# In-place block products in a gated linear attention scan, and a weight check ordered behind the last unit's masks

## The chip, the cores and the metric

The kernel runs on one core of one Trainium2 chip. The metric is device time in microseconds (us): 799.12 us is the median of five runs of the kernel before (797.18 to 802.22). The engines are named as in the profile: PE (matmul), PEld (its weight loads), DVE (the vector engine), ACT (the scalar engine), POOL and SP (here used mostly to issue DMAs).

## The reference

A gated linear attention with a complex decay gives `x`, and a feed-forward block with a squared ReLU follows.

```python
mag = sqrt(a_re**2 + a_im**2); scale = min(mag, 0.999) / (mag + 1e-6)
ar, ai = a_re * scale, a_im * scale            # (B, H, S, D) = (4, 8, 768, 48)
for t in range(S):                             # state (B, H, D, D), complex
    S_re, S_im = ar[t]*S_re - ai[t]*S_im + outer(k[t], v[t]), ar[t]*S_im + ai[t]*S_re
    y[t] = q[t] @ S_re
x = y.transpose(0, 2, 1, 3).reshape(3072, 384)
out = maximum(x @ w_in, 0)**2 @ w_out          # w_in 384 x 2048, w_out 2048 x 384, float64
```

The two weight matrices arrive as 64-bit floats and are lowered to float32 on the chip.

## The kernel before, in words

**Units.** The 3072 rows are cut into 8 units of 384 rows (4 batches, 2 halves each), `u["n"]` 0 to 7. Each unit passes three stages.

- `chain_work`: loads `a`, `q`, `k`, `v`; normalises the gates (`roots`, `normalise`); multiplies them within groups of 3 rows (`inner`, 128 groups per unit); `totals` transposes the 128 group products with PE (tile `tot`) into the tile `e`, which is 128 partitions by (2 parts, 3 chunks of channels, 129 places). `scan` then turns the 128 places into running complex products. `back` transposes them back with PE (tile `bk`), ACT copies them to `xn`, and `apply` multiplies them into the gates, giving `QK`.
- `pair_work`: for each of 4 pairs of heads `turn` (PE transposes `tq`, ACT copies to `QKT`), `score` (PE `sa`, DVE multiplies by the mask into `A`), `keep` (PE `kv`, DVE sums the states into `St` and `S`), `mix` (PE `ypair`, ACT copies to `yt`, SP issues the DMAs into `xT`).
- `hidden_work` (PE `h`, ACT squares into `g`) and `project_work` (PE `o`, ACT copies to `ot`, SP stores).

**The scan before** (lines 814 to 838). `product` (line 796) is one complex multiplication in four DVE operations: two multiplications over both parts (line 808) into the scratch tiles `fa0`, `fa1`, one subtraction (811), one addition (812). `scan` views the 128 places as 32 blocks of 4. Three products make the running products inside the blocks (`v4`, stride of 4 elements in memory). The 32 block ends are copied into a small tile (`inc`, line 822) and scanned there: three products inside 8 groups of 4, three doubling steps over the 8 group ends, three products (one per chunk) to bring the group ends in. Three more products, again one per chunk, multiply all 4 places of blocks 1 to 31 by the end of the block before. That is 15 products and a copy: 61 operations. One unit in two adds a small carry product into `ce`.

**The weight check.** The range of the 64-bit weights is checked in 32 pieces during the last unit's dense stage. `look(i)` issues a DMA of a piece (384 KB) through POOL into one of four scratch tiles; `inspect(i)` masks its high words (line 635) and takes their maximum (line 637), then calls `look(i + 4)`. `verdict` gathers all checks; one PE matmul (`cnt`, line 1058) and one DVE operation make the flag that decides, at the very end, whether a slower general path has to run.

**Order.** `merge` interleaves the lists of work of neighbouring units: the dense stage of unit n, the pairs of unit n+1, the chain of unit n+2. What is written there is only a priority: a scheduler with its own estimates of durations sets the order of the instructions on every engine when the program is built, and each engine then runs its own queue strictly in that order. `after(x, y)` adds an order between two instructions to that scheduler and no semaphore. The first unit has no stage before it, so its chain runs alone at the start.

## Time and profile before

The profiled execution took 795.03 us, with a span of 793.3 us from the first to the last instruction, at a mean granted TensorE clock of 0.991.

| engine | busy us | share of the span | instructions |
|---|---|---|---|
| PE | 716.8 | 90% | 3538 |
| PEld | 467.2 | 59% | 3538 |
| DVE | 517.4 | 65% | 1340 |
| ACT | 400.7 | 51% | 754 |
| POOL | 110.3 | 14% | 162 |

Busy shares are averages over stages with different limits: PE does almost nothing in the first 40 us, then is nearly full. A row of the timeline reads: start, duration in us, engine, line, operation, output and input tiles, their sizes, and in brackets the idle time before it with what ended it. One fp32 matmul of the program appears as two records in the trace.

### The profile page before, as it was taken

How to read it: one execution, taken by the hardware profiler on the slowest of the kernel's cores; microseconds unless marked ns; L12 is line 12 of the kernel's file. 1: busy time of each engine (PE TensorE's matmuls, PEld its weight loads, DVE VectorE, ACT ScalarE, POOL GpSimd, SP SyncE). 2: the span in 40 equal slices, each digit the busy share in tenths (PEclk: the TensorE clock that was granted, in tenths of full speed). 3: DMA queues.
4: the chain of work that ended last, by engine and by line, in shares of the span. 5: the costliest groups of instructions: out<-in, count | busy, mean ns of one | idle time of the engine just before them, and what ended most of it. 6: DMA issues, size and time to landing. Idle time of an engine off the chain costs nothing.

```text
span 793.3 us, 10047 instructions
## 1 busy us (share of the span) xinstructions
PE 716.8 (90%) x3538; PEld 467.2 (59%) x3538; DVE 517.4 (65%) x1340; ACT 400.7 (51%) x754; POOL 110.3 (14%) x162
## 2 busy tenths in 40 slices
PE   0169799899899999999999999999899999899997
PEld 0047455567455666766566666666566666565553
DVE  5899889887988985688654858287655867510000
ACT  5825388067667439911993149621982145212510
POOL 4004100031040022002300050003200144100000
PEclk9999999999999999999999999999999999999999
DMA  9429440061051034003600071004500188500000
GB/s 277 161 69 321 139 148 11 14 226 45 16 199 51 26 112 162 9 19 93 210 8 9 29 236 30 16 18 130 167 8 18 58 275 285 169 18 28 0 11 25
DMA packets 38748, 76.25 MB, mean 96 GB/s; under 512 B 10752, under 2 KB 25216, under 8 KB 38688
## 3 DMA queue, kind: packets, MB, share of 16 engines
q0 software_dynamic: 14608, 55.85, 21.4%
q1 hardware_dynamic: 24080, 19.67, 8.3%
q8 instruction: 30, 0.49, 0.3%
q14 instruction: 30, 0.25, 0.1%
HBM read 56.62 MB, written 14.16 MB: 89 GB/s over the span
## 4 chain that ended last, share of the span: by engine, by line
PE 31%; issue 21%; DVE 8%; DMA 7%; ACT 7%; POOL 1%; SPq 0%; POOLq 0%; ACTq 0%
PE o L1012 15%; PE h L998 8%; DMA a<-in_a_im_dram 3%; PE sa L927 2%; DVE fa L808 2%; DMA look<-in_moe_w_out_dram 2%; PE ypair L963 1%; PE ypair L968 1%; PE kv L944 1%; DMA look<-in_moe_w_in_dram 1%; ACT QKT L918 1%; PE tq L917 1%; DMA rows<-QK 1%; ACT fa L677 1%; ACT g L1003 1%
## 5 line engine op out<-in xcount | busy, mean ns | idle before, releaser
L998 PE MATMUL h<-xT,w 128*128 128x384 f32 x768 | 265.1, 489 | 5.2 <-DMA xT<-yt 4.7
L1012 PE MATMUL o<-w,g 128*128 128x384 f32 x768 | 266.6, 492 | 0.0
L998 PEld LDWEIGHTS h<-xT,w 128*128 128x128 f32 x768 | 139.2, 191 | 87.5 <-issue 8.9
L1012 PEld LDWEIGHTS o<-w,g 128*128 128x128 f32 x768 | 140.8, 192 | 84.1 <-issue 4.9
L918 ACT COPY QKT<-tq 96x512 f32<-96x512 f32 x96 | 78.6, 855 | 28.3 <-PE tq L917 28.3
L1003 ACT ACTIVATE g<-h 128x384 f32<-128x384 f32 x128 | 61.7, 484 | 61.0 <-PE h L998 60.6
L1004 ACT ACTIVATE g<-g 128x384 f32<-128x384 f32 x128 | 66.6, 522 | 2.3
L929 DVE TENSOR_TENSOR A<-sa,mask 128x384 f32<-128x384 f32 x64 | 35.4, 553 | 44.9 <-PE sa L927 44.4
L917 PE MATMUL tq<-ident,QK 128*96 128x128 f32 x384 | 57.6, 278 | 6.0 <-ACT QKT L918 5.7
L917 PEld LDWEIGHTS tq<-ident,QK 128*96 128x96 f32 x384 | 44.4, 129 | 29.0 <-issue 11.8
L927 PEld LDWEIGHTS sa<-QKT 96*128 96x128 f32 x384 | 50.5, 193 | 17.1 <-ACT QKT L918 8.1
L927 PE MATMUL sa<-QKT 96*128 96x128 f32 x384 | 56.1, 284 | 4.7 <-ACT QKT L918 4.6
L1016 ACT COPY ot<-o 128x384 f32<-128x384 f32 x24 | 11.4, 474 | 86.9 <-PE o L1012 84.6
L971 ACT COPY yt<-ypair 112x384 f32<-112x384 f32 x32 | 15.3, 477 | 77.3 <-PE ypair L968 70.9
L1059 DVE TENSOR_SCALAR flag<-cnt 1x1 int32<-1x1 f32 x1 | 0.1, 148 | 68.4 <-PE cnt L1058 68.4
L779 PE MATMUL tot<-ident,last 128*128 128x128 f32 x72 | 14.4, 301 | 29.8 <-ACT last L739 26.2
L963 PE MATMUL ypair<-A,v 128*48 128x128 f32 x384 | 39.1, 282 | 0.3 <-ACT yt L971 0.3
L663 POOL DMA_DIRECT2D v<-in_v_dram x18 | 16.0, 893 | 156.4 <-issue 122.8
L896 POOL DMA_DIRECT2D rows<-QK x16 | 9.2, 574 | 203.8 <-DVE QK L888 164.7
L944 PEld LDWEIGHTS kv<-v,KC 128*96 128x96 f32 x320 | 31.6, 167 | 8.6 <-ACT QKT L918 4.0
L677 ACT ACTIVATE fa<-a 128x1152 f32<-128x1152 f32 x16 | 18.6, 1160 | 35.2 <-DMA a<-in_a_im_dram 35.2
L944 PE MATMUL kv<-v,KC 128*96 128x48 f32 x320 | 32.5, 248 | 2.7 <-DMA KC<-rows 1.5
(117 smaller groups left out, 964.1 us busy)
## 6 DMA issues: line engine op xcount, KB each, us to landing
rows<-QK POOLq DMA_DIRECT2D x16, 576.0 KB, 4.9
raw<-in_moe_w_in_dram POOLq DMA_DIRECT2D x16, 384.0 KB, 6.1
look<-in_moe_w_in_dram POOLq DMA_DIRECT2D x16, 384.0 KB, 4.1
look<-in_moe_w_out_dram POOLq DMA_DIRECT2D x16, 384.0 KB, 4.3
KC<-rows POOLq DMA_DIRECT2D x8, 576.0 KB, 5.0
out_dram<-ot SPq DMA_DIRECT2D x24, 192.0 KB, 1.9
raw<-in_moe_w_out_dram SPq DMA_DIRECT2D x11, 384.0 KB, 3.9
xT<-yt SPq DMA_DIRECT2D x48, 72.0 KB, 2.2
```

What stands on the lines that cost most here:

```text
L663: get.dma_start(out=u["v"][:, j], in_=src(v).rearrange("h (j s) d -> s j h d", s=C)[:, j])
L677: square = act.activation(out=whole(fa), in_=whole(a), func=AF.Square, accum_out=sums[:, n, z:z + 1])
L917: nc.tensor.transpose(ps[:, 2 * j + h], src, ident)
L918: act.copy(out=u["T"][i].rearrange("r z (p c) -> r c z p", c=W)[:, c], in_=ps)
L927: nc.tensor.matmul(sa[:, j], lhsT=T[:, 2 + h, ts(j, C)], rhs=T[:, h, ts(j, C)], start=True, stop=True)
L929: dve.tensor_tensor(out=u["A"][i][:, h], in0=sa, in1=mask3, op=ALU.mult)
L944: nc.tensor.matmul(ps[:, j, h], lhsT=u["KC", hh // HH][:, j, hh % HH], rhs=u["v"][:, j, hh], start=True, stop=True)
L963: nc.tensor.matmul(ypair[64 * h:64 * h + D, ts(j, C)], lhsT=u["v"][:, j, 2 * i + h], rhs=A[:, h, j], start=True, stop=S_j is None)
L998: nc.tensor.matmul(ps, lhsT=w1[:, f, m], rhs=u["xT"][:, m], start=(m == 0), stop=(m == NM - 1))
L1003: act.activation(out=t, in_=ps, func=AF.Relu)
L1004: act.activation(out=t, in_=t, func=AF.Square)
L1012: nc.tensor.matmul(u["o"], lhsT=u["g"][f][:, ts(c, C)], rhs=w2[:, f], start=(f == 0), stop=(f == NF - 1))
```

## The change

There are three edits. The scan is done in place in `e`, without `inc`: a first product joins blocks of 4 to blocks of 8 (16 block ends, a stride of 8 elements), four doubling steps run over the 16 ends, one product repairs the 16 left ends, and one product over all three chunks multiplies the first 3 places of blocks 1 to 31 by the end of the block before. That last product has too many dimensions for one operand, so its multiplications are issued per part: 4 multiplications, a subtraction and an addition. Together that is 42 operations. Second, the first operation of every `inspect` is ordered behind the last mask multiplication and the last state sum that were recorded. Third, for unit 0 the copy of the first state (4 copies, one per pair of heads) is done by ACT and not by DVE.

```diff
         hi = looks.pop(i)
-        dve.tensor_scalar(out=hi, in0=hi, scalar1=0x38000000, scalar2=0x78000000,
+        first = dve.tensor_scalar(out=hi, in0=hi, scalar1=0x38000000, scalar2=0x78000000,
                           op0=ALU.bitwise_xor, op1=ALU.bitwise_and)
+        for x in ("A", "S"):
+            after(first, mark[x])
...
-            dve.tensor_tensor(out=t, in0=x, in1=y[:, j].unsqueeze(1).to_broadcast(shape),
-                              op=ALU.mult)
+            if len(shape) < 5:
+                dve.tensor_tensor(out=t, in0=x, in1=y[:, j].unsqueeze(1).to_broadcast(shape),
+                                  op=ALU.mult)
+            else:
+                for r in range(2):
+                    dve.tensor_tensor(out=t[:, r], in0=x[:, r], in1=y[:, j], op=ALU.mult)
...
         for w in range(1, 4):
             product(u, v4[:, :, :, :, w], v4[:, :, :, :, w - 1], v4[:, :, :, :, w])
-        inc = whole(u["fb", 0])[:, 0:2 * NM * 32].rearrange("p (r m g) -> p r m g", r=2, m=NM)
-        i4 = inc.rearrange("p r m (k w) -> p r m k w", w=4)
-        dve.tensor_copy(out=inc, in_=v4[:, :, :, :, 3])
-        for w in range(1, 4):
-            product(u, i4[:, :, :, :, w], i4[:, :, :, :, w - 1], i4[:, :, :, :, w])
-        top = i4[:, :, :, :, 3]
-        for step in (1, 2, 4):
-            product(u, top[:, :, :, step:8], top[:, :, :, step:8], top[:, :, :, 0:8 - step])
-        for m in range(NM):
-            product(u, i4[:, :, m, 1:8, 0:3], i4[:, :, m, 1:8, 0:3],
-                    top[:, :, m, 0:7].unsqueeze(3).to_broadcast([C, 2, 7, 3]))
-        for m in range(NM):
-            product(u, v4[:, :, m, 1:32], v4[:, :, m, 1:32],
-                    inc[:, :, m, 0:31].unsqueeze(3).to_broadcast([C, 2, 31, 4]))
+        v8 = e[:, :, :, 0:C].rearrange("p r m (g w) -> p r m g w", w=8)
+        left, right = v8[:, :, :, :, 3], v8[:, :, :, :, 7]
+        product(u, right, right, left)
+        for step in (1, 2, 4, 8):
+            product(u, right[:, :, :, step:16], right[:, :, :, step:16],
+                    right[:, :, :, 0:16 - step])
+        product(u, left[:, :, :, 1:16], left[:, :, :, 1:16], right[:, :, :, 0:15])
+        product(u, v4[:, :, :, 1:32, 0:3], v4[:, :, :, 1:32, 0:3],
+                v4[:, :, :, 0:31, 3].unsqueeze(4).to_broadcast([C, 2, NM, 31, 3]))
...
-        dve.tensor_tensor(out=u["A"][i][:, h], in0=sa, in1=mask3, op=ALU.mult)
+        mark["A"] = dve.tensor_tensor(out=u["A"][i][:, h], in0=sa, in1=mask3, op=ALU.mult)
...
-            if before is None:
+            if before is None and u["n"] == 0:
+                act.copy(out=outs[j], in_=ps[:, j])
+            elif before is None:
                 dve.tensor_copy(out=outs[j], in_=ps[:, j])
             else:
-                dve.tensor_tensor(out=outs[j], in0=ps[:, j], in1=before, op=ALU.add)
+                mark["S"] = dve.tensor_tensor(out=outs[j], in0=ps[:, j], in1=before,
+                                              op=ALU.add)
```

The order that the scheduler makes of the changed program differs in these places. On DVE all 32 inspections now follow the last unit's last state sum. On PE the queue differs up to unit 3 and is the same from there to the end, `cnt` included (in front of the last 8 `o` matmuls of the program). In unit 1 the transposes `tot` and `bk` stand further back in the row of `o` matmuls (10 in place of 4 before the first `tot`, 35 in place of 31 before the first `bk`), and the six `bk` of `e` stand together, where before other matmuls lay between them; in unit 2 the first `bk` of `e` stands 1 matmul earlier. In unit 0 two and not three `h` matmuls stand before the last `ypair`. On POOL one `look` moves from in front of the last `KC` load to behind it. On ACT the four copies of unit 0 stand among the `raw` conversions.

## The prediction

> **What bounds the kernel now.** I read the busy table and the slices first, then the stretches of 20 us, the waits of PE, and around each of its waits the timelines of DVE and PE.

> ```profile
> PE   0169799899899999999999999999899999899997
> PEclk9999999999999999999999999999999999999999
> ```

> PE is nearly full from the fourth slice (60 us) to the end, so it bounds the kernel from there, and DVE counts only where PE waits for it. Before that it is idle. The stretches (columns: PE, PEld, DVE, ACT, POOL busy with counts, granted clock, DMA share, GB/s) show who is not:

> ```profile
> 20.00:40.00 20.00, 2.94 (x9) 1.48 (x9) 17.98 (x55) 16.20 (x31) 0.60 (x2) 1.00 0.48 156
> 40.00:60.00 20.00, 14.10 (x56) 9.75 (x57) 18.62 (x59) 5.57 (x10) 0.54 (x1) 1.00 0.25 78
> 140.00:160.00 20.00, 17.59 (x60) 10.85 (x59) 17.09 (x66) 1.82 (x4) 1.50 (x2) 0.91 0.11 35
> 680.00:700.00 20.00, 17.70 (x81) 11.10 (x80) 7.33 (x19) 4.46 (x7) 1.17 (x2) 0.91 0.28 92
> ```

> DVE bounds the start: unit 0's scan runs alone. In 140 to 160 and 680 to 700 PE has holes at a clock of 0.91. PE's waits (total, times, longest) and timeline name them:

> ```profile
> PE bk L844 <- DVE e L811: 19.1, 6, 12.4
> PE ypair L968 <- DVE St L954: 2.3, 1, 2.3
> ```
> ```profile
> 148.05 0.66 PE L844 MATMUL bk<-ident,e 128*128 128x128 f32 x2 [2.41 <-DVE e L811]
> 148.50 1.49 PE L1012 MATMUL o<-w,g 128*128 128x384 f32 x2
> ...
> 683.57 0.60 PE L968 MATMUL ypair<-QKT,St 96*48 96x128 f32 x4 [2.29 <-DVE St L954]
> ...
> 684.95 3.90 PE L1012 MATMUL o<-w,g 128*128 128x384 f32 x8
> ...
> 689.36 2.75 PE L1012 MATMUL o<-w,g 128*128 128x384 f32 x8
> ```

> `bk` waits for the end of a scan: 12.4 us at the start, 2.41 at 148, 2.53 at 213, 0.60 at 276; for units 4 to 7 PE reaches `bk` after the scan is done and waits for nothing. At 681 PE waits 2.29 us for a state sum that stands on DVE behind inspections, which wait for `look` DMAs; the next eight `o` records then take 3.90 us in place of 2.75.

> **The scan, step by step.** Rows of DVE by form (busy us, mean ns):

> ```profile
> L808 DVE TENSOR_TENSOR fa<-e 128x192 f32<-128x192 f32 x48 | 22.5, 504 | 13.0 <-ACT e L781 12.5
> L808 DVE TENSOR_TENSOR fa<-e,fb 128x248 f32<-128x248 f32 x48 | 17.8, 412 | 0.7
> L808 DVE TENSOR_TENSOR fa<-fb 128x42 f32<-128x42 f32 x64 | 10.6, 208 | 1.1
> L808 DVE TENSOR_TENSOR fa<-fb 128x48 f32<-128x48 f32 x48 | 9.7, 239 | 0.7
> ```

> Operands that lie together: 248 elements 412 ns, 576 elements about 751 ns (line 735), so 1.03 ns per element, 443 ns for 279. Operands in steps of 4 elements (16 bytes): 48 take 239 ns, 192 take 504, so 1.84 ns per element. The outputs in such steps (line 811: 96 elements 334 ns, 24 elements 201) grow by 1.85. Runs of 3 out of 4 pay nothing extra: the 42 mix both kinds, 229 ns in the doubling steps and 200 in runs of 3, as 1.84 and 1.03 per element would give.

> No row shows a step of 8 elements (32 bytes), which 24 of the new operations have. The lower bound of its price is that of operands lying together (1.03), the upper one the 16-byte price with its surcharge doubled (2.65); I take 1.84, the nearest row. [...]

> A product takes two multiplications and two half-size operations, less 0.12 us of overlap; with 48 elements 2 x 0.239 + 0.201 + 0.195 - 0.12 = 0.75, and the timeline has 0.76 (36.59 to 37.35). New: the join of 96 elements 1.02, steps of 90, 84, 72, 48 elements 0.99, 0.95, 0.89, 0.75, the left ends (90) 0.99: 5.59 us. The last product: four multiplications of 279 elements, 4 x 0.443 - 0.21 = 1.56, subtraction 0.36, addition 0.45: 2.37. Together 7.96. Old, same place: from the copy at 36.23 to the end of the last addition at 46.77, 10.54. Saved: 2.6 us per scan. The steps of 8 hold 1440 elements, so the high price saves 1.4 and the low one 3.7.

> **What it moves.** *Start:* all of unit 0 hangs on this chain. `bk` of the real part now waits for the one subtraction, and six `bk` come together, some 0.2 us: 2.4 us earlier.

> *Unit 0's pairs, 62 to 96 us:* DVE (18.66 and 16.70 of 20 busy) loses four copies of 0.25 us. ACT has room (10.48 and 7.46 of 20); a copy of this size is not shown there, the nearest take 0.35 (line 740) and 0.48 (971), and it stands behind `raw` conversions, one of which waited 0.45 us for a DMA. Gain 0 to 1.0, I take 0.5. The third `h` no longer stands before the last `ypair`; before, it held that `ypair` back 1.30 us (for `xT`).

> *Unit 1, 126 to 170 us:* PE waits 0.90 for `tot` and 2.41 for `bk`. One `o` of the program is two records, 0.65 us. `bk` now stands 4 of them later, 2.6 us, so PE would reach it, without waits, at 145.64 - 2.4 - 0.5 - 0.9 + 2.6 = 144.4. DVE ends the subtraction at 140.14 (end of the third product) + 5.59 + 2.00, less its own 2.4 and 1.0, so 144.3. The wait goes. With it goes the slow stretch after it: two `o` records took 1.28 instead of 0.65, four 1.79 instead of 1.29, `bk` 0.2 more, 1.35 us. Then DVE is next: its part from the first use of `xn` (152.82) to the last line-883 operation (166.74) is unchanged at 13.9 us, with less of `o` to fill PE's gaps; I take 0.5 us back. At 170 us PE is 2.9 + 0.9 + 2.4 + 1.35 - 0.5 = 7.0 us earlier; 0.5 for the uncertain clock off: 6.5.

> *Units 2 and 3:* the first `bk` of unit 2 stands 0.65 us earlier and needs the whole last product, where before it needed a third of it (2.6 us less). PE is there at 211.13 - 7.0 - 0.65 = 203.5, DVE's subtraction ends at 205.72 + 5.59 + 2.00 - 7.0 = 206.3: a wait of 2.8 for 2.53, 0.3 lost. In unit 3 half of the 0.60 goes, 0.3 gained. *Units 4 to 7:* nothing; PE's own arrival at `bk` sets `apply`, and the waits of 1.9, 1.49 and 1.66 us at 395, 483 and 571 are for ACT, behind loads.

> *The end:* with the inspections behind the last state sum, the hole at 681 goes. From 680.41 to 688.69 PE took 8.28 us; the same groups at 705.05 to 709.19 took 4.14. Gain 4.1. What is moved: 28 of the 32 `look` DMAs (384 KB each) issue after 714 and not from 640; POOL has nothing behind them, the `KC` load gets free of one. SP's last `xT` transfers, issued 720.5 and 721.1, meet them: 2.1 us to landing alone, 4.4 at 665.9 under looks, so 725.5 where the first `h` starts at 725.12: 0.5 lost. Net 3.6. [...]

> The cover of the inspections:

> ```profile
> 713.56 0.25 DVE L954 TENSOR_TENSOR St<-kv,St 96x96 f32<-96x96 f32 x1
> 782.20 0.15 DVE L1059 TENSOR_SCALAR flag<-cnt 1x1 int32<-1x1 f32 x1 [68.38 <-PE cnt L1058]
> ```

> DVE is empty from 714 to 782, where `cnt` needs the verdict: 68 us. Before, the 32 took 52.4 us (635.2 to 687.6). They fit.

> Sum: 6.5 - 0.3 + 0.3 + 3.6 = 10.1 us. The profiled execution took 795.03; it becomes 784.9. The median of the runs is 4.1 us above the profiled one, so the forecast for the median is 789.0.

> **The rivals.** *A, the middle gives it back:* `bk` stands together and PE's queue is fixed, so PE could wait in units 1 and 2 for the whole last product. For it: the 2.53 us at 213 that I do not remove. Against it: the 2.6 us of `o` put before `bk` in unit 1. Start 2.4 and end 3.6 remain, less 1.0 in each unit: 4.0 us, 795.1.

> *B, the step of 32 bytes is dear:* the scan saves 1.4 and not 2.6. Two scans stand before unit 1's `bk`, so 2.4 us less: 7.7, 791.4. For it: step 16 already costs 0.8 ns per element more. Against it: steps of 8 bytes (line 607, 384 elements, 549 ns) pay nothing, so the cost is a threshold and not a slope.

> *C, slower: the inspections end after `cnt`.* Then PE stands in front of its last 8 `o`. It decides at 68.2 / 32 = 2.13 us per inspection; before it was 1.64. One buffer's round is a landing (4.2 us) and some 1.5 us of issue and two operations, shared by four buffers; with the 9.5 us that POOL's `raw` loads from `w_out` took to land it would be 11 / 4 = 2.75, 88 us in all, a wait of 20 us on PE: 10 us slower than before, 809. Against it: from 713 on the DMA share is 0.08 or less, so the looks are nearly alone.

> **How the numbers follow.** Forecast 0.71, A 0.17, B 0.07, C 0.05. 0.5%, or 4.0 us, is about what a measurement of this kernel can tell from no change, so the border lies at 795.1. A sits on it (0.05 faster, 0.12 same); forecast and B are faster. Faster 0.83, same 0.12, slower 0.05. Low end: the scan's low price in the two scans (2.2), and the 1.71 us at 233 and the 0.9 of clock and `xT` I took off: 784.2. High end: A with the high price of the scan at the start, 1.2 more: 796.3. C is left out.

> **What would show it.** Right: `bk` of unit 0 starts near 42 and the first line-861 operation near 45.2; the new operations of 96 elements take about 0.33 us and those of 279 about 0.44; no wait of `bk` near 144; no wait of `ypair` for `St` near 670; the last inspection ends near 760, over 10 us before `cnt`. Wrong: 96 elements over 0.4 us (B); waits for `bk` of 2 us or more in units 1 and 2 together with an unchanged time at 215 (A); `cnt` waiting for `good` (C); waits of PE for ACT that grow in units 4 to 7, which I hold unchanged.

## The result and the profile after

The kernel after takes 791.76 us (median of 27 runs, 789.09 to 797.95), the kernel before 799.24 us beside it (48 runs); the ratio is 0.9915, 95% interval 0.9898 to 0.9931. The forecast was 789.0 with a range of 784.2 to 796.3: the sign and the range hold, but of 10.1 us only about 7 came. The profiled execution took 790.50 us (span 788.7, granted clock 0.987) against 795.03, a difference of 4.5 us; why this pair shows less than the medians is part of what follows. The ratio leaves out runs that took over 1.5% more than the fastest of their kernel; the differences of means below take all runs, and without those few the changed kernel stands 6.3 ± 0.9 us (and not 6.6 ± 0.9) below before. Lines of the kernel after line 636 stand two to six higher than before.

The slices of the page, as shown for the kernel before:

```profile
PE   0178899899899999999989999999899999999997
PEclk9998899999999999999999999999999999999999
```

Two slices, 60 to 100 us, have a lower clock than before; the slice at 680 us has no dent any more. The operations of the new scan on DVE by form (busy us, mean ns):

```profile
L815 DVE TENSOR_TENSOR fa<-e 128x279 f32<-128x279 f32 x32 | 12.2, 444 | 0.0
L811 DVE TENSOR_TENSOR fa<-e 128x90 f32<-128x90 f32 x32 | 8.8, 319 | 0.5
L811 DVE TENSOR_TENSOR fa<-e 128x96 f32<-128x96 f32 x16 | 4.6, 329 | 0.2
L817 DVE TENSOR_TENSOR e<-fa,fa 128x24 f32<-128x24 f32 x8 | 1.6, 202 | 0.3
```

The step of 8 elements costs what the step of 4 costs: 96 elements take 329 ns (taken: 327), and as outputs 24 elements take 202 ns (201 in steps of 4). The 279 take 444 ns (taken: 443). From the join to the last addition the scan of unit 0 takes 7.82 us, from 36.61 to 44.43; 7.96 was forecast, 10.54 it was. The waits of PE (total, times, longest) and its timeline:

```profile
PE bk L846 <- DVE e L817: 17.8, 3, 12.1
PE h L1003 <- DMA xT<-yt: 3.7, 4, 1.7
PE ypair L973 <- DVE St L958: 0.3, 1, 0.3
```
```profile
62.12 1.22 PE L946 MATMUL kv<-v,KC 128*96 128x48 f32 x12 [1.50 <-DMA KC<-rows]
...
95.55 27.33 PE L1003 MATMUL h<-xT,w 128*128 128x384 f32 x84 [1.73 <-DMA xT<-yt]
...
130.49 0.44 PE L781 MATMUL tot<-ident,last 128*128 128x128 f32 x2 [1.16 <-ACT last L741]
...
150.83 1.51 PE L846 MATMUL bk<-ident,e 128*128 128x128 f32 x6 [2.80 <-DVE e L817]
...
213.09 0.84 PE L846 MATMUL bk<-ident,e 128*128 128x128 f32 x6 [2.92 <-DVE e L817]
...
681.07 0.39 PE L973 MATMUL ypair<-QKT,St 96*48 96x128 f32 x4
681.39 2.85 PE L1017 MATMUL o<-w,g 128*128 128x384 f32 x8
```

Three things are to be seen. The first `kv` of unit 0 starts at 62.12, 2.75 us earlier than before (64.87), but the long run of `h` starts at 95.55 where it started at 95.73: in this pair of profiles the gain of the start is gone by then. Unit 1 still waits 2.80 us for `bk`. The hole at 681 is closed: `ypair` follows without a wait, and the next eight `o` records take 2.85 us, where they took 3.90.

Where the start was lost shows in stretches of 10 us, first the kernel after, then before (columns as above: granted clock third from the right):

```profile
70.00:80.00 10.00, 9.54 (x53) 7.54 (x53) 7.44 (x20) 4.07 (x7) 2.28 (x3) 0.59 0.76 245
80.00:90.00 10.00, 9.73 (x68) 6.90 (x66) 4.18 (x13) 4.43 (x9) 0.00 (x0) 0.73 0.08 22
```
```profile
70.00:80.00 10.00, 9.66 (x99) 7.90 (x98) 9.19 (x25) 6.04 (x11) 4.61 (x6) 1.00 0.98 312
80.00:90.00 10.00, 8.04 (x57) 5.30 (x56) 7.82 (x23) 3.66 (x7) 0.42 (x1) 0.83 0.11 31
```

After, PE ran at 0.59 and 0.73, and DVE (7.44 and 4.18 busy) waited for PE. Summed over stretches of 5 us, (1 - clock) x 5, PE lost 6.8 us of clock between 60 and 100, before 3.45. (The clock records of both traces are 1.00 or 0.50, nothing between, so 3.4 us at 0.50 are a loss of 1.7.)

The end of DVE's work (the last inspection, and the flag):

```profile
753.67 0.55 DVE L639 TENSOR_REDUCE odd<-look 128x1 f32<-128x384 uint32 x1
...
777.59 0.15 DVE L1064 TENSOR_SCALAR flag<-cnt 1x1 int32<-1x1 f32 x1 [22.76 <-PE cnt L1063]
```

The inspections end at 754, over 22 us before the flag.

### The profile page after: what moved, and what is told of

Same layout as the page of the kernel before. It is cut to its first block, busy times and chain, and to the rows that moved or that the text cites. A ratio compares the mean times of both kernels' runs of the same rounds, so it can differ in the third digit from the quotient of the medians.

```text
span 788.7 us, 9897 instructions
## 1 busy us (share of the span) xinstructions
PE 715.5 (91%) x3538; PEld 469.0 (59%) x3538; DVE 499.8 (63%) x1184; ACT 400.7 (51%) x758; POOL 111.0 (14%) x162
## 4 chain that ended last, share of the span: by engine, by line
PE 39%; DVE 12%; issue 11%; ACT 8%; DMA 4%; POOL 1%; ACTq 0%; POOLq 0%
PE o L1017 19%; PE h L1003 10%; DMA a<-in_a_im_dram 3%; PE sa L929 3%; PE kv L946 2%; PE ypair L968 2%; PE tq L919 2%; DVE QK L890 1%; DVE fa L717 1%; ACT QKT L920 1%; PE ypair L973 1%; DVE fa L811 1%; DVE a L705 1%; DMA rows<-QK 1%; ACT fa L679 1%
## 5 line engine op out<-in xcount | busy, mean ns | idle before, releaser
L929 PE MATMUL sa<-QKT 96*128 96x128 f32 x384 | 57.8, 289 | 3.1 <-ACT QKT L920 2.9
L811 DVE TENSOR_TENSOR fa<-e 128x192 f32<-128x192 f32 (+6 forms) x152 | 48.7, 358 | 14.5 <-ACT e L783 12.5
L781 PE MATMUL tot<-ident,last 128*128 128x128 f32 x72 | 14.4, 301 | 30.3 <-ACT last L741 26.9
L968 PE MATMUL ypair<-A,v 128*48 128x128 f32 x384 | 39.8, 283 | 1.0 <-ACT yt L976 1.0
L847 ACT COPY xn<-bk 128x384 f32<-128x384 f32 x24 | 11.4, 480 | 50.0 <-PE bk L846 50.0
```

Of the source, the lines that this page charges most:

```text
L811: dve.tensor_tensor(out=t, in0=x, in1=y[:, j].unsqueeze(1).to_broadcast(shape), op=ALU.mult)
L929: nc.tensor.matmul(sa[:, j], lhsT=T[:, 2 + h, ts(j, C)], rhs=T[:, h, ts(j, C)], start=True, stop=True)
L968: nc.tensor.matmul(ypair[64 * h:64 * h + D, ts(j, C)], lhsT=u["v"][:, j, 2 * i + h], rhs=A[:, h, j], start=True, stop=S_j is None)
```

## The experiments

The theory on record: start 2.4 us, unit 1 some 4, end 3.6. The rival formed on the trace: the start is lost before 96 us, unit 1 gives nothing, the end gives the bulk. A difference "of means" below is between all runs of two kernels, with its 95% interval: 117 of before (mean 798.95), 39 of after (792.34; after - before = -6.6 ± 0.9). The 17 runs of before beside e11 came later; with them it is -6.5 ± 0.9. "At equal clock" means that each run's lost clock, (1 - granted clock) x span, is taken off its time. That is somewhat too much, since a part of it falls where PE has nothing to do (in after the last slow stretch begins at 785.2 us, PE's last record ends at 782.9), but it takes a third to a half off the scatter. So counted, after stands 5.0 ± 0.6 us below before (the 86 runs of before beside the experiments).

### One part at a time

```diff
 e1: the kernel before with the new product() and scan() only
 e2: the kernel before with
+        for x in ("A", "S"):
+            after(first, mark[x])
```

> The kernel before with the new scan alone; no ordering of the weight inspections, state copies of unit 0 on DVE. The theory on record gives the scan 2.4 us at the start, 0.9 + 2.4 + 1.35 - 0.5 in unit 1, less some clock: about 6 us faster than before (ratio near 0.9925), with the hole at 681 us still there. The rival, formed on the trace of the changed kernel: what the scan gives is gone by 96 us, in a stretch at half clock between 72 and 85 us, and unit 1's wait for bk stays; then 0 to 3 us faster (ratio 0.996 to 1.000).

> The kernel before with the inspections ordered behind the last masks and state sums, and nothing else. The theory on record gives the end 3.6 us (ratio 0.9955) and no change before 640 us. The rival, in which the end is the bulk of the gain of 6.8 us and the scan gives little, has 4 to 6 us here (ratio 0.992 to 0.995).

Measured: e1 797.85 us, ratio 1.0003 (0.9973 to 1.0032), by means -0.6 ± 2.1 us against before; e2 794.24 us, ratio 0.9944 (0.9917 to 0.9971), by means -5.1 ± 1.5 us (at equal clock -2.4 ± 1.2, about the wait of 2.29 us at 681; the rest is clock). The ordering alone holds the larger part of the gain. The scan alone gives nothing that can be told (at equal clock -0.5 ± 0.9 us), and not the 6 us of the theory; the rival's 0 to 3 us hold. PE and DVE of e1 at the old hole:

```profile
685.61 0.67 PE L968 MATMUL ypair<-QKT,St 96*48 96x128 f32 x4 [3.66 <-DVE St L954]
...
687.06 4.68 PE L1012 MATMUL o<-w,g 128*128 128x384 f32 x8
```
```profile
684.45 0.36 DVE L635 TENSOR_SCALAR look<-look 128x384 uint32<-128x384 uint32 x1 [0.51 <-DMA look<-in_moe_w_out_dram]
684.85 0.55 DVE L637 TENSOR_REDUCE odd<-look 128x1 f32<-128x384 uint32 x1
685.32 0.24 DVE L954 TENSOR_TENSOR St<-kv,S 96x96 f32<-96x96 f32 x1
```

The order on DVE is that of before: 14 inspections stand between this state sum and the ones ahead of it, in both kernels. They waited longer for their `look` transfers here (7.0 us in all against 5.3), so PE's wait is 3.66 us and not 2.29, and 3.4 us of clock are lost from 680 to 695, where before lost 1.7. But PE came to this hole at 681.95, in before at 681.28, with 1.7 us more of lost clock behind it: in this profile what the scan brought at the start was gone ahead of the hole. Where it goes in e1 is not shown. Nor do the times show that the two parts fail to add: -0.6 ± 2.1 and -5.1 ± 1.5 against -6.6 ± 0.9 for the whole change.

### The state copies

```diff
-            if before is None and u["n"] == 0:
-                act.copy(out=outs[j], in_=ps[:, j])
-            elif before is None:
+            if before is None:
                 dve.tensor_copy(out=outs[j], in_=ps[:, j])
```

> The changed kernel with the state copies of unit 0 back on DVE: new scan and ordering stay. On record the copies on ACT are worth 0.5 us, between 0 and 1.0, so this is 0.5 us slower than the changed kernel (ratio 0.992). The rival: in the changed kernel the second copy stood on ACT behind a conversion that waited 4.4 us for a weight DMA, and PE's waits after it were followed by 12 us at half clock; without that this one is 2 to 4 us faster than the changed kernel (ratio 0.987 to 0.989), and its granted clock between 70 and 90 us is above 0.8.

Measured: 791.79 us, by means -0.2 ± 1.4 against the changed kernel (at equal clock +1.6 ± 1.2). Neither theory is confirmed: 0.5 us lies inside the interval, and the rival's 2 to 4 us of gain fall, though its mark on the clock is there (0.83 from 70 to 90). Against e2 the same kernel is at -1.7 ± 1.9 (at equal clock -1.0 ± 1.6): with the copies on DVE no run shows a worth of the scan that stands clear of noise. But the trace shows a side effect that I had not priced:

```profile
125.04 0.44 PE L781 MATMUL tot<-ident,last 128*128 128x128 f32 x2 [0.82 <-ACT last L741]
```

Here unit 1's first `tot` comes 30.7 us after the long run of `h` began (94.32). In all five profiles without copies on ACT this is 30.3 to 31.0, in all nine with them 34.4 to 37.5. Moving four copies of 0.25 us to ACT let the scheduler set up the whole chain of unit 1 some 4 us later. In its order before (line 700, first row) and after (the other rows) one sees how:

```profile
116.18 0.76 DVE L700 SCALAR_TENSOR_TENSOR fa<-fa 128x576 f32<-128x576 f32 x1 [0.58 <-ACT fa L699]
```
```profile
118.65 0.76 DVE L687 SCALAR_TENSOR_TENSOR fb<-fb 128x576 f32<-128x576 f32 x1 [1.79 <-ACT fb L686]
119.44 0.76 DVE L689 SCALAR_TENSOR_TENSOR fb<-fb,fa 128x576 f32<-128x576 f32 x1
120.59 0.76 DVE L702 SCALAR_TENSOR_TENSOR fa<-fa 128x576 f32<-128x576 f32 x1 [0.39 <-ACT fa L701]
```

The first half's step (line 700 before, 702 after) stands behind the second half's roots, which wait 1.79 us for ACT: 120.59 and not 116.18. It comes 25.0 us after the long `h` began, before 20.5; e3 has the order of before, and there it is 20.4. For the time this matters little: the scheduler puts 30 `o` of the program in front of unit 1's `bk` in e1 and e3 and 35 in the changed kernel, so PE does other work meanwhile and waits 2.76, 2.74 and 2.80 us.

### What the start is worth

```diff
 e4:
-    scan = new in all units
+    scan = old in unit 0, new in units 1 to 7
 e5, ahead of the last product of unit 0's scan:
+        for _ in range(10):
+            product(u, idle, right, left)
```

> The changed kernel with the old scan in unit 0 only. On record the start is worth 2.4 us and, as unit 1's part is to wait for PE and not for DVE, nearly all of it reaches the end: 2 to 2.5 us slower than the changed kernel (ratio 0.994 to 0.995). The rival (the start's gain is used up before 96 us, where hidden(0) waits for its xT transfers): within 0.7 us of the changed kernel (ratio 0.991 to 0.992), first h run near 95.6 as in both kernels.

> The changed kernel itself once more, as the base of the other runs on the same chip: ratio to before 0.990 to 0.993, as it had (0.9915).

> The changed kernel with ten idle products of 96 elements before the last product of unit 0's scan; no instruction changes its place otherwise. They take 10 x 1.02 = 10.2 us on the chain at the start. The theory on record (all of unit 0 hangs on this chain, up to the end of the kernel): 9 to 10.5 us slower than the changed kernel (ratio to before about 1.004), and the first long run of h near 105.7 instead of 95.6. The rival (the loads of the weights, or the slow clock between 62 and 96 us, set when hidden(0) starts, and that is where the 2.4 us went): at most 6 us slower (ratio up to 0.999).

Measured: e4 794.20 us, +2.7 ± 1.5 against the changed kernel by means (at equal clock +4.1 ± 1.0), so its rival, within 0.7 us, falls. The changed kernel again (c_after) 791.97 us, beside which e5 has 801.33 us, 9.4 us more by medians, +8.8 ± 1.65 by means over all runs of the changed kernel (at equal clock +9.6 ± 1.1). The profile of e5:

```profile
53.44 1.51 PE L850 MATMUL bk<-ident,e 128*128 128x128 f32 x6 [21.63 <-DVE e L817]
...
104.45 27.33 PE L1007 MATMUL h<-xT,w 128*128 128x384 f32 x84 [2.00 <-DMA xT<-yt]
```

`bk` starts 9.4 us later than in c_after (44.00), so the idle products cost 9.4 us, and 9.4 reach the end. The rival falls: neither the loads nor the slow clock swallows a change of the start. Then why did the two profiles meet at 96 us? Because each has its own amount of slow clock. The first `kv` starts at 61.8 to 62.8 in the ten profiles with the new scan in unit 0 (e5 left out) and at 64.9 to 65.1 in the three with the old one, 2.7 us apart on average. The long run of `h` starts at 93.4 to 96.5 and at 95.7 to 99.7, on average 95.0 and 97.2. In between they lost 3.4 us of clock (e6, e6b, e8) to 6.8 (e10, e11). The changed kernel lost 6.8 in both of its profiles, before 3.45 in its one.

### Unit 1

```diff
 e6 (and e6b, the same again), in front of unit 1's bk:
+            if u["n"] == 1:
+                after(op, mark["o"])        # the 40th o of unit 0 and not the 35th
     (10 steps of unit 0's project_work are built ahead of the last 5 of unit 1's chain_work)
 e8: e6, with the state copies of unit 0 on DVE
 e7, in front of bk in units 1 and 2:
+            for _ in range(16):
+                after(nc.tensor.transpose(ps[:, 0], ident, ident), mark["join"])
 e11: old scan in unit 1, new in the others
 e10: old scan in units 2 to 7, new in units 0 and 1
```

> The changed kernel with five more o of the program (3.25 us) in front of unit 1's bk, where PE waited 2.80 us for the subtraction of the last product. If DVE's chain sets unit 1 up to its QK (its 13.9 us after bk are unchanged), the wait only moves behind bk, in front of tq: the same time within 1 us. If PE's own work after bk sets it, the 2.8 us and the 1.7 us of slow clock that came after them go: 3 to 4.5 us faster than the changed kernel (ratio 0.986 to 0.988).

> The kernel of e6 (five more o in front of unit 1's bk) a second time, since its first comparison left 0 to 4 us open. If the wait only moved behind bk, the median lies within 1 us of the changed kernel's 791.8; if it went, at 787 to 789.

> As e6, but with the state copies of unit 0 back on DVE. In the profiles without the copies on ACT the first tot of unit 1 comes 30.3 to 30.8 us after the first long run of h, with them 34.4 to 37.5, and the scheduler puts 30 and not 35 o in front of bk; here it is 40 behind the earlier chain. If unit 1's chain on DVE sets the time, the earlier chain is worth 2 to 4 us: 787 to 789. If PE's work does, no wait of PE for bk and the same time as e6 within 1 us.

Measured: e6 789.91 and 788.90 us, together -2.0 ± 1.5 against the changed kernel by means; e8 789.27 us, -2.4 ± 1.9. Both beat before (e6 by 8.6 ± 1.4) and, by little, the changed kernel. e8 is no faster than e6, so the earlier chain alone brought nothing that can be told. The trace of e6:

```profile
93.38 27.33 PE L1005 MATMUL h<-xT,w 128*128 128x384 f32 x84 [1.71 <-DMA xT<-yt]
...
149.76 0.82 PE L846 MATMUL bk<-ident,e 128*128 128x128 f32 x6
...
194.45 1.53 PE L1005 MATMUL h<-xT,w 128*128 128x384 f32 x4 [2.19 <-DMA xT<-yt]
```

The wait for `bk` is gone, and a wait of 2.19 us for `xT` has taken its place. From the start of the long `h` to the end of the span e6 takes 692.5 us, e6b 693.5, e8 692.5, the changed kernel 693.2 and 692.3: about the same, with 1.7, 5.1 and 0 us of lost clock in it, in the changed kernel twice 1.7. What these kernels are ahead in their profiles lies before 94 us, where they lost 3.4 us of clock and the changed kernel 6.8.

For e6 the edit can't be the cause of that: up to 144 us PE, DVE, ACT and POOL have the same order in the changed kernel, e6, e6b, e7, e10 and e11. What differs between their seven profiles is where the points in time lie at which the clock can change (see the last section). The clock records begin, at full clock, 47.2 to 48.3 us after the start of the span in the five profiles that lost 6.8 us (two of the changed kernel, e7, e10, e11), and at 50.2 and 50.0 in e6 and e6b. That reads as the chance of the execution. At equal clock the 14 runs of e6 stand at -0.7 ± 0.9 us against the changed kernel and e8 at +1.0 ± 1.2. So the wait moved, as the first theory of e6 had it, and a gain by the edit itself is not shown.

> The changed kernel with sixteen idle transposes of the identity on PE (16 x 0.28 = 4.5 us) in front of bk of units 1 and 2, where PE waited 2.8 and 2.9 us; the real bk overwrites their output. If the 1.7 us at half clock that stand after such waits in five of six profiles come from the idle time of PE, these records vanish behind 150 us with no wait of PE left there, and the time is 0 to 2 us lower in spite of the useless work. If the slow clock has another cause (a beat of its own), the clock after 150 us drops as before and the time is 2 to 4 us higher.

Measured: 794.25 us, +1.9 ± 1.5 (at equal clock +2.9 ± 1.0). It did not test what it should:

```profile
146.15 1.91 PE L849 MATMUL bk<-ident 128*128 128x128 f32 x16
150.91 0.90 PE L851 MATMUL bk<-ident,e 128*128 128x128 f32 x6 [2.85 <-DVE e L818]
```

The sixteen took 1.91 us, not 4.5, and the scheduler took three `o` (1.95 us) from in front of `bk` for them; the hole stayed. Nor did c_after, with a hole of 2.71 us at the same place, lose clock there.

> The changed kernel with the old scan in unit 1 only. On record unit 1 gives 4.1 of the 10.1 us (its wait for bk, the slow clock behind it, the wait for tot, less 0.5), which need its new scan to end 2.6 us sooner: without it 2.5 to 4 us slower than the changed kernel (ratio 0.994 to 0.997). The rival, from the two profiles: in the changed kernel PE waits 2.8 us for bk of unit 1 as before, so nothing of it was had, and the old scan, whose first transposes need only a third of the last product, brings bk no more than 0.3 us later: the same time within 1 us (ratio 0.990 to 0.993).

> The changed kernel with the old scan in units 2 to 7 and the new one in units 0 and 1. On record those scans are worth 0.3 lost and 0.3 gained in units 2 and 3 and nothing behind: the same time as the changed kernel within 1 us (ratio 0.990 to 0.994). The rival: DVE's lighter load in units 2 to 7 shortens PE's waits for ACT and DVE behind 200 us, and 2 to 3 us of the gain come from there (ratio 0.994 to 0.996).

Measured: e11 797.90 us, +6.1 ± 1.5, on a chip where before had 797.15 beside it; e10 793.14 us, +0.9 ± 1.6. At equal clock these are +5.2 ± 0.9 and +0.1 ± 1.3. In e10 the scans of units 2 to 7 are worth nothing that can be told, as on record. e11 was a surprise: in the changed kernel the new scan in unit 1 is worth all of 6 us. Its trace, and the same row of c_after below:

```profile
152.15 0.44 PE L873 MATMUL bk<-ident,e 128*128 128x128 f32 x2 [3.04 <-DVE e L817]
...
200.60 2.17 PE L1030 MATMUL h<-xT,w 128*128 128x384 f32 x6 [1.35 <-DMA xT<-yt]
...
204.38 0.33 PE L781 MATMUL tot<-ident,last 128*128 128x128 f32 x1 [1.17 <-ACT last L742]
...
206.30 0.91 PE L1030 MATMUL h<-xT,w 128*128 128x384 f32 x2 [1.59 <-ACT g L1035]
```
```profile
198.11 2.17 PE L1003 MATMUL h<-xT,w 128*128 128x384 f32 x6 [0.71 <-DMA xT<-yt]
```

From the long `h` of unit 0 to this `h` of unit 1 e11 needs 104.9 us, c_after 101.6; two more waits of 1.17 and 1.59 us follow at 204 and 206. The kernel before, however, has 103.3 us with 1.7 of lost clock in it, so 101.6 as well, and e2 (old scan, copies on DVE) 103.0 with 1.7, so 101.3. In these profiles only the old scan together with copies on ACT is slow. That reads as two edits that cancel in unit 1: the copies on ACT push the chain back by some 4 us, and the shorter scan fetches that back. It is not shown: the old scan in unit 1 alone, with the copies on DVE, was not run, and behind 152 us the order on PE in e11 is another than in the changed kernel too.

## Why the prediction was right or wrong

**The scan's price: right.** 7.82 us against 7.96, and the rival of a dear 32-byte step is refuted (329 ns, not over 400).

**The start, 2.4 us: right.** The first `apply` operation starts at 45.64 (45.2 forecast), `kv` 2.75 us earlier. Undoing it costs 2.7 ± 1.5 us, and a delay of 9.4 us reaches the end as 9.4 by medians. The marker of `bk` was wrong: I wrote "near 42", but all six wait for the one subtraction, which by my own terms ends at 36.23 + 5.59 + 2.00 = 43.8; they start at 44.22.

**Unit 1, about 4 of the 10.1 us: wrong, and this is where the missing part is.** The step that failed is "DVE ends the subtraction at 140.14 (end of the third product) + 5.59 + 2.00, less its own 2.4 and 1.0, so 144.3. The wait goes." I let the third product end as it did before, moved only by the start. It ended at 143.2, with the long `h` at the same time as before, and the subtraction ended at 150.7:

```profile
142.85 0.33 DVE L818 TENSOR_TENSOR e<-fa,fa 128x96 f32<-128x96 f32 x1
...
150.23 0.45 DVE L817 TENSOR_TENSOR e<-fa,fa 128x279 f32<-128x279 f32 x1
```

PE was ready for `bk` at 148.03, and not at 144.4. I had counted the four `o` that the scheduler put in front of `bk` as cover. They were its answer to a chain that it had itself set later: the first `tot` had moved back by six `o` in the same order, and I did not follow that to DVE. With the copies on DVE the chain is not late, but then fewer `o` stand in front of `bk` (30), and the wait is the same (e1, e3). The clock behind the wait (1.35) and the wait for `tot` (0.9) stayed with it.

**The four copies, 0.5 us: not resolved** as such (e3 against the changed kernel: -0.2 ± 1.4, at equal clock +1.6 ± 1.2), but mis-sized in kind. I priced them as 0.25 us each and not as an edit that reorders the chain of the next unit.

**Units 2 to 7, nothing: right** (e10; `bk` of unit 2 waits 2.92, forecast 2.8; the wait for ACT at 571 us stays, 2.12 us).

**The end, 3.6 us: right, perhaps a little small.** From the `ypair` at 679.93 to the `sa` behind the eight `o`, at 684.07, PE takes 4.14 us where it took 8.28; the 0.5 for late `xT` was not paid, since PE had `o` until the first `h` of unit 7 at 720.51 and did not wait. The ordering alone gives 5.1 ± 1.5, which just holds the 3.6, and from the long `h` to the end the changed kernel takes 4.4 and 5.3 us less than before. The late inspections are hidden: they end 22 us before the flag, so rival C is refuted.

**Rival A** had its marks: waits of 2.80 and 2.92 us in units 1 and 2, and `bk` of unit 2 at 213.09 where it stood at 213.66. Its mechanism, PE waiting for the whole last product, is the one that worked in unit 1. Its price was too low: the start and the end, 2.4 + 3.6, make 6.0 us, and 6.6 ± 0.9 was measured; the further 1.0 that it took off in each of units 1 and 2 was too much, as the two waits grew by 0.4 us each (2.41 to 2.80, 2.53 to 2.92). The median, 791.8, lies between the forecast (789.0) and A (795.1); it fell into the range, with unit 1 read wrongly, because the range had taken in A.

**The offset.** I put the forecast 4.1 us above the profiled sum, as the median before lies. The profiled run of after lies 1.3 us under its median. Single executions differ by slow clock, so a pair of profiles, 4.5 us apart, told less of the gain than the medians.

## What to carry to other kernels

When a scheduler places the instructions, read the moves of all rows of a stage together: work that turns up in front of a wait can mean that the thing waited for has been set later, and then it covers nothing. An edit worth a microsecond on one engine may reorder the chain of the next unit; price it by its new order and not by its instructions. What a part is worth can depend on its company: the scan alone gave nothing that could be told, the ordering 5 us, the whole change 6.6, and undoing the scan in one unit cost 6. And where runs differ by their clock, compare them at equal clock as well: here that told the effect of an edit from the luck of an execution.

## What the runs showed of the hardware

The slow clock comes in pieces. In the clock records of before and after every slow stretch lasts 3.41 us, but for one of four times that (13.65 us, from 71.8 in after) and for the last of each, which the end cuts; the clock in it is 0.50. In c_after two last some 6.8 us (from 71.3 and 81.6). So a loss is 1.7 us or a multiple: 1.7 at 145 to 155 (before) and at 150 (after), 3.4 in e1's hole, 6.8 between 70 and 90 in both profiles of the changed kernel. It follows waits of PE, but not each: the same changed kernel lost 1.7 us after its `bk` wait of 2.80 us at 150 in one profile, and in the other none after 2.71 us there but 1.7 at 395. The waits that were followed by slow records are shorter than one such piece (2.06 us before the loss at 395, 2.29 at 681, 2.80 at 150), so here a wait of less than two thirds of it was enough at times.

Between 60 and 100 us PE lost 3.4 us (before, e6, e6b, e8) to 6.8 us (after, c_after, e10, e11) in this way, which is as much as the edits were worth.
